# Clustered attention and spatial gating on one core: simple steps moved between ScalarE, VectorE and PSUM, and a new planned order

## The chip, the cores and the metric

The kernel runs on one core of a Trainium2 chip. The metric is the device time of one execution in microseconds; the kernel before takes 690.79 us (median of 3 runs, 690.44 to 691.78).

## What is computed

Attention in which a query sees only the keys of its own cluster, and on its output a spatial gating layer. Batch 4, 8 heads, 768 positions, head dimension 64, 16 clusters; model width 512, inner width 1024, of which u and v are 512 each. Everything goes in and out as float32.

```python
q_assign = argmax(q_n @ c_n)            # q_n, k_n, c_n: rows of unit length
k_assign = argmax(k_n @ c_n)
scores = where(q_assign == k_assign, scale * q @ k.T, -1e9)
attn = softmax(scores);  x = attn @ v   # heads side by side: [4, 768, 512]
h = relu(x @ w_in);  u, v = h[..., :512], h[..., 512:]
v_n = (v - mean(v)) / sqrt(var(v) + 1e-6)
v_s = w_spatial @ v_n + b_spatial
out = (u * v_s) @ w_out
```

## The kernel before, in words

TensorE works on float16. So that results stay close to float32, most operands are split into a high part (the value cast to float16) and a low part (what the cast lost), and products are summed from high x high, high x low and low x high.

**Pairs of heads.** The work is cut into 16 pairs of heads, four for each batch. For pair n, `prep(n)` loads keys and queries (`raw`) and values (`vraw`), splits them (ScalarE makes `hq`, line 532; VectorE subtracts to `lo`, line 538; for values lines 601 and 606), multiplies with the centroids (lines 553 to 555) and turns the products into one-hot rows on VectorE (lines 566 to 571). Two VectorE operations scale the one-hots by a penalty and write them as float16 into `ohx` (lines 577 and 578); a DMA transpose and row copies on SyncE's queue put them below the keys and queries in `hq`, so that the score matmul itself adds the mask. Sums over the values (line 621 or 613) are split into `wh` (VectorE, line 630), `w` (line 631) and `wl` (ScalarE, line 632).

`shifts(n)` multiplies scores a first time (line 662) only for their maxima, which VectorE reduces out of PSUM (line 669, 18 reductions a pair), and puts the negated maxima into further rows of `hq` (lines 680 to 684, through ScalarE, whose bias at 684 is read from a tile `flag`).

`attend(n)` goes over 2 heads x 6 key tiles: scores into a PSUM tile of 768 columns (lines 713 and 715), exp on ScalarE with a bias read from the tile `plog` (line 719, float32 `p`), the cast to float16 on ScalarE (line 721), the low part on GpSimd (line 722, one instruction over 768 columns), and the product with the values (line 727). Lines 746 to 751 normalise a head's result and split it into `xhl`; a DMA transpose makes `xT`.

**The gating layer.** `mlp(b)` follows when the four pairs of a batch are there, beside the pairs of the next batch. All its matmuls are at line 771: x with w_in to v (line 792, its statistics at 798 to 809, normalised at 811, cast to float16 by VectorE at 812, low part by GpSimd at 813) and to u (line 822); w_spatial with v_n; VectorE multiplies with u (line 832) and casts (line 833), GpSimd makes the low part (line 834), a DMA transposes it to `gT`; the product with w_out leaves through ScalarE (line 842).

**Weights.** w_in comes in eight pieces of 512 columns. It is stored as two words for each element; three VectorE operations put a word together in a PSUM accumulator (lines 477 to 479, `acc`), then ScalarE casts (line 461) and VectorE subtracts (line 462). w_out comes in eight pieces of 256 columns that take the same steps with the words put together in SBUF (`top`). w_spatial comes as float32 in twelve pieces of 384 columns.

**Order.** Nothing is issued as it is written. Each operation is entered in a plan with an engine, a cost, what it comes after, a key and in part a due time (line 195 on). `Plan.run` steps through time: whichever engine is free takes, of the operations that could start by then, the one with the lowest due time (or start) plus key, and the instruction is emitted. Each engine's queue thus has a fixed order. Four PSUM accumulators of 512 columns (`acc`) are shared by maxima, products with centroids, sums, attention results, the gating layer and w_in's words; two of 1024 (`sc`) hold scores.

Of the kernel before, what the change touches and what calls it, by code (L numbers as in the profile page):

```python
# [7 lines left out]
F32 = mybir.dt.float32  # L8
# [43 lines left out]
MM = 6  # L52
W_KEY = 7.7
WL_KEY = 0.91
WL_AT = 183.98
WL_GAP = 3.25
W_AT = 28.34
W_GAP = 5.52
PREP_KEY = 2.81
AV_KEY = 1.09  # L60
K_SC = -2.4
K_MX = -2.81
K_MAX = -0.27

TBL = 0.14
K_SH = -3.11
K_EXP = 0.71
K_HI = -1.78
K_LO = 2.77
K_RC = -1.64  # L70
K_XD = 3.66
K_X = -1.98
K_VT = -3.58
K_G = -9.5
KP0 = -16.99
KC = -30.0
# [44 lines left out]
class Op:  # L121
    __slots__ = ("eng", "cost", "fn", "after", "order", "new", "claim", "key", "at", "dma", "turn", "cols", "due", "left", "ready", "outs", "end", "seq", "alt", "s", "free")
# [14 lines left out]
class Plan:  # L137
# [24 lines left out]
    def run(self):
# [47 lines left out]
        while done < len(self.ops):  # L210
# [29 lines left out]
            if o.dma is None:  # L240
# [35 lines left out]
def kernel(  # L276
# [75 lines left out]
    r_wraw = R(wk, "wraw", [P, 512], F32, 2)  # L352
# [48 lines left out]
    m_half = op("DVE", 0.2, lambda: (V.memset(half, 0.5), V.memset(mhalf, -0.5), V.memset(plog, P_LOG * LN2), V.memset(flag[:, 0:1], -1.0), V.memset(flag[:, 1:2], -(2.0 ** -MEAN_LOG)), [V.memset(x[:, :, 2:3], LIM) for x in nms]), key=-9)  # L401
# [50 lines left out]
    def weights(jobs, at, gap, key, raws, tops, on, after=()):  # L452
        ends = []
        for m, (src, dst, n, lg, wide, cell) in enumerate(jobs):
# [4 lines left out]
            def lows(x, ld, n=n, dst=dst, sc=sc, raw=raw, cell=cell, use=()):  # L459

                h = op("ACT", 0.2 + 0.00085 * n, lambda: A.activation(out=dst()[:, 0, :], in_=x(), func=AF.Copy, scale=sc), after=ld, use=use, key=key)
                lo = op("DVE", (0.05 if n > 384 else 0.4) + 0.00125 * n, lambda: V.scalar_tensor_tensor(out=dst()[:, 1, :], in0=x(), scalar=sc, in1=dst()[:, 0, :], op0=ALU.mult, op1=ALU.subtract), after=[h], use=use, key=key)
                w_ops.setdefault(cell, []).extend([h, lo])
                ends.append(lo)
# [12 lines left out]
            x1 = op("DVE", (0.1 if n > 256 else 0.3) + 0.0011 * n, lambda raw=raw, top=top, n=n: V.tensor_scalar(out=top.t.bitcast(U32), in0=words(raw, n, 1), scalar1=3, scalar2=0x3FFFFFFF, op0=ALU.logical_shift_left, op1=ALU.bitwise_and), after=[ld], use=[raw], new=[top], key=key)  # L477
            x2 = op("DVE", (0.05 if n > 256 else 0.35) + 0.00125 * n, lambda raw=raw, top=top, n=n: V.scalar_tensor_tensor(out=top.t.bitcast(U32), in0=words(raw, n, 1), scalar=0xC0000000, in1=top.t.bitcast(U32), op0=ALU.bitwise_and, op1=ALU.bitwise_or), after=[x1], use=[raw, top], key=key)
            x3 = op("DVE", (0.05 if n > 256 else 0.35) + 0.00125 * n, lambda raw=raw, top=top, n=n: V.scalar_tensor_tensor(out=top.t.bitcast(U32), in0=words(raw, n, 0), scalar=29, in1=top.t.bitcast(U32), op0=ALU.logical_shift_right, op1=ALU.bitwise_or), after=[x2], use=[raw, top], key=key)
            lows(lambda top=top: top.t, [x3], use=[top])  # L480
# [35 lines left out]
    def prep(n):
        plan.due = due(n, DUE_PREP) if n else None
# [15 lines left out]
        for h, ld in enumerate(raws):  # L533
            if n == 1:
                o = op("ACT", 0.83, lambda h=h: A.activation(out=raw.t[:, h, :], in_=raw.t[:, h, :], func=AF.Copy, scale=QK_SCALE), after=[his[h]], use=[raw], key=KP)
                los.append(op("POOL", 1.7, lambda h=h: G_.tensor_tensor(out=lo.t[:, h, :], in0=raw.t[:, h, :], in1=hq.t[:, 0, h, :], op=ALU.subtract), after=[o], use=[raw, hq] + ([lo] if h else []), new=[] if h else [lo], key=KP))
                continue
            los.append(op("DVE", 1.4 if n else 0.96, lambda h=h: V.scalar_tensor_tensor(out=lo.t[:, h, :], in0=raw.t[:, h, :], scalar=QK_SCALE, in1=hq.t[:, 0, h, :], op0=ALU.mult, op1=ALU.subtract), after=[his[h]], use=[raw, hq] + ([lo] if h else []), new=[] if h else [lo], key=KP))  # L538
# [38 lines left out]
        k1 = op("DVE", 0.32, lambda: V.tensor_scalar(out=ohxv[:, :, 0:2], in0=oh2(0), scalar1=PEN, scalar2=None, op0=ALU.mult), after=[o_oh, last.get("oht"), c_oh], use=[misc], key=KP)  # L577
        k2 = op("DVE", 0.32, lambda: V.tensor_scalar(out=ohxv[:, :, 2:4], in0=oh2(1), scalar1=PEN, scalar2=-PEN, op0=ALU.mult, op1=ALU.add), after=[o_oh, last.get("oht"), c_oh], use=[misc], key=KP)
# [335 lines left out]
```

## Time and profile before

| what | value |
|---|---|
| median of 3 runs | 690.79 us (690.44 to 691.78) |
| the profiled execution: span from first to last instruction | 692.5 us |
| mean granted TensorE clock | 0.985 |
| TensorE busy | 637.5 us, 92% |
| VectorE busy | 482.0 us, 70% |
| ScalarE busy | 437.7 us, 63% |
| GpSimd busy | 435.3 us, 63% |
| read from HBM, written | 27.63 MB, 6.29 MB |

The profiled execution is one of its own and is not among the three runs; its span alone is above their median. In the profile's rows PE is TensorE, DVE VectorE, ACT ScalarE, POOL GpSimd and SP SyncE. A row of a group gives line, engine, operation, output and inputs with their shapes and the count; then busy time and the mean of one in ns; then the engine's idle time before them and what ended it. The chain of waits follows the work back from the last instruction, at each step to what released it. A row of the table over stretches gives the stretch, then each engine's busy time in it with its instructions, the granted TensorE clock, the share of the DMA engines and GB/s. Matmuls are pipelined and their ends modelled.

### The profile page before, as it was taken

To read this page: it belongs to the slowest core of one execution; us is meant where nothing else is said; L and a number is where in the kernel's file an instruction comes from. 1 tells how busy PE (TensorE), PEld (TensorE's weight loads), DVE (VectorE), ACT (ScalarE), POOL (GpSimd) and SP (SyncE) were. 2 spreads that over 40 slices of the span, in tenths; PEclk is the share of its full clock that TensorE was granted. 3 is DMA by queue.
4 is the path that set the end of the run, shared out by engine and by line. 5 is a ranking of instruction groups with operands and counts; after the bars stand their busy time and mean duration, and the time that the engine had idled before them with its cause. 6 is when DMAs were issued, how large, how long until landed. Compare 5 with 4: busy or idle time off the path is not lost.

```text
span 692.5 us, 16725 instructions
## 1 busy us (share of the span) xinstructions
PE 637.5 (92%) x6757; PEld 379.0 (55%) x6757; DVE 482.0 (70%) x940; ACT 437.7 (63%) x685; POOL 435.3 (63%) x305
## 2 busy tenths in 40 slices
PE   2978889999998999988799899999999999999996
PEld 1456566666555655555445556556655655544442
DVE  6999989998969889999754877558485821215210
ACT  5686889998848756678443966667673957412111
POOL 2485778998949667677363976767665966703210
PEclk9998999999999799999999999999999999999999
DMA  5567665574634467442831536262510113140223
GB/s 165 147 154 213 147 107 142 137 168 116 138 110 82 97 165 167 109 116 60 189 61 36 150 74 137 61 152 50 120 34 1 37 28 70 32 115 0 31 61 92
DMA packets 106515, 70.49 MB, mean 102 GB/s; under 512 B 90379, under 2 KB 93126, under 8 KB 106438
## 3 DMA queue, kind: packets, MB, share of 16 engines
q1 hardware_dynamic: 102694, 62.74, 40.4%
q10 hardware_dynamic: 3744, 6.69, 2.7%
q8 instruction: 53, 0.87, 0.5%
q14 instruction: 24, 0.20, 0.1%
HBM read 27.63 MB, written 6.29 MB: 49 GB/s over the span
## 4 chain that ended last, share of the span: by engine, by line
PE 60%; DVE 20%; ACT 9%; issue 5%; DMA 4%; POOL 2%; POOLq 0%; SPq 0%; ACTq 0%; DVEq 0%
PE acc L771 35%; PE acc L727 9%; DVE nm L669 8%; PE acc L662 6%; PE sc L713 5%; PE sc L715 5%; ACT p L719 4%; ACT pt L721 3%; DVE lo L538 2%; POOL pt L722 2%; DMA out_dram<-o 2%; DMA gT<-ghl 1%; ACT hq L532 1%; DVE vhl L606 1%; DVE acc L568 1%
## 5 line engine op out<-in xcount | busy, mean ns | idle before, releaser
L722 POOL TENSOR_TENSOR pt<-p,pt 128x768 f16<-128x768 f32 x192 | 329.7, 1736 | 103.1 <-ACT pt L721 50.6
L719 ACT ACTIVATE p<-sc,plog 128x768 f32<-128x768 f32 x192 | 168.9, 898 | 58.4 <-PE sc L715 53.8
L669 DVE TENSOR_REDUCE nm<-acc 128x1 f32<-128x512 f32 (+1 forms) x288 | 179.8, 683 | 12.4 <-PE acc L662 12.0
L721 ACT CAST pt<-p 128x768 f16<-128x768 f32 x192 | 155.6, 828 | 12.9 <-PE acc L727 11.1
L727 PE MATMUL acc<-vhl,pt 128*128 128x65 f16 (+1 forms) x3456 | 139.2, 196 | 7.6 <-POOL pt L722 6.9
L727 PEld LDWEIGHTS <-pt 128*128 128x128 f16 x3456 | 129.1, 99 | 30.3 <-POOL pt L722 10.1
L771 PE MATMUL acc<-win,xT 128*128 128x512 f16 x576 | 130.0, 379 | 0.0
L662 PE MATMUL acc<-hq 80*128 80x256 f16 (+1 forms) x384 | 101.1, 339 | 20.7 <-DVE nm L669 10.1
L713 PE MATMUL sc<-hq,lo 128*128 128x512 f16 (+1 forms) x384 | 95.7, 331 | 6.3 <-ACT p L719 6.1
L715 PE MATMUL sc<-hq 81*128 81x512 f16 (+1 forms) x384 | 96.0, 331 | 1.0 <-DMA hq<-sht 1.0
L771 PE MATMUL acc<-vn,wsp 128*128 128x512 f16 x432 | 96.8, 379 | 0.0
L771 PEld LDWEIGHTS <-xT 128*128 128x128 f16 x576 | 54.9, 98 | 63.2 <-issue 0.7
L771 PEld LDWEIGHTS <-wsp 128*128 128x128 f16 x432 | 41.8, 98 | 48.9 <-issue 0.2
L834 POOL TENSOR_TENSOR ghl<-u,ghl 128x512 f16<-128x512 f32 x24 | 27.7, 1156 | 64.0 <-DVE ghl L833 49.2
L832 DVE SCALAR_TENSOR_TENSOR u<-acc,bsp,u 128x512 f32<-128x512 f32 x24 | 17.9, 747 | 71.5 <-PE acc L771 71.5
L771 PE MATMUL acc<-wou,gT 128*128 128x512 f16 x288 | 65.6, 379 | 1.7 <-DMA gT<-ghl 1.7
L662 PEld LDWEIGHTS <-hq 80*128 80x128 f16 x384 | 35.3, 99 | 43.2 <-issue 25.1
L538 DVE SCALAR_TENSOR_TENSOR lo<-raw,hq 128x768 f16<-128x768 f32 x30 | 44.9, 1505 | 12.4 <-ACT hq L532 12.0
L713 PEld LDWEIGHTS <-lo 128*128 128x128 f16 x384 | 34.1, 98 | 34.9 <-issue 20.8
L715 PEld LDWEIGHTS <-hq 81*128 81x128 f16 x384 | 37.9, 99 | 27.7 <-issue 2.7
L842 ACT ACTIVATE o<-acc 128x512 f32<-128x512 f32 x24 | 14.3, 597 | 57.0 <-PE acc L771 41.2
L771 PEld LDWEIGHTS <-gT 128*128 128x128 f16 x288 | 27.7, 98 | 33.8 <-DMA gT<-ghl 2.2
(111 smaller groups left out, 628.5 us busy)
## 6 DMA issues: line engine op xcount, KB each, us to landing
raw<-in_kqT_dram SPq DMA_DIRECT2D x15, 768.0 KB
vraw<-in_vp_dram SPq DMA_DIRECT2D x16, 384.0 KB
out_dram<-o ACTq DMA_DIRECT2D x24, 256.0 KB
hq<-hq SPq DMA_DIRECT2D x15, 384.0 KB
vn<-in_w_in_dram SPq DMA_DIRECT2D x8, 512.0 KB
hq<-lo SPq DMA_DIRECT2D x16, 192.0 KB
lo<-hq SPq DMA_DIRECT2D x16, 192.0 KB
wraw<-in_wsT_dram SPq DMA_DIRECT2D x12, 192.0 KB
```

Source lines behind the costliest of these rows:

```text
L538: los.append(op("DVE", 1.4 if n else 0.96, lambda h=h: V.scalar_tensor_tensor(out=lo.t[:, h, :], in0=raw.t[:, h, :], scalar=QK_SCALE, in1= ...
L662: T.matmul(out=acc.t[:, c:c + cs.stop - cs.start], lhsT=hq.t[0:R_SH, 1, h, t * P:(t + 1) * P], rhs=hq.t[0:R_SH, 0, h, cs], start=c == 0, s ...
L669: V.tensor_reduce(out=nm.t[:, t, k:k + 1] if n == 1 else nm.t[:, t:t + n, k], in_=src, axis=AX.X, op=ALU.max, negate=True)
L713: T.matmul(out=sc.t[:, cs], lhsT=lo.t[:, h, ks], rhs=hq.t[:, 2, h, cs], start=True, stop=False)
L715: T.matmul(out=sc.t[:, cs], lhsT=hq.t[0:R_E, 0, h, ks], rhs=hq.t[0:R_E, 1, h, cs], start=False, stop=True)
L719: o = op("ACT", 0.9, lambda sc=sc, p32=p32: A.activation(out=p32.t, in_=sc.t[:, 0:S], func=AF.Exp, bias=plog, scale=SC_UNIT), after=[o, m_ ...
L721: o = op("ACT", 0.83, lambda pt=pt, p32=p32: A.copy(out=pt.t[:, 0, :], in_=p32.t), after=[o], use=[p32], new=[pt], key=K_HI)
L722: o = op("POOL", 1.72, lambda pt=pt, p32=p32: G_.tensor_tensor(out=pt.t[:, 1, :], in0=p32.t, in1=pt.t[:, 0, :], op=ALU.subtract), after=[o ...
L727: T.matmul(out=av.t[:, t * (D + 1):t * (D + 1) + w], lhsT=lhsT, rhs=rhs, skip_group_check=True, **f)
L771: T.matmul(out=acc.t, lhsT=lr[m][0], rhs=lr[m][1], start=(m == 0), stop=(m == n - 1))
L832: o = op("DVE", 0.72, lambda: V.scalar_tensor_tensor(out=u32.t, in0=acc.t, scalar=bsp[:, t:t + 1], in1=u32.t, op0=ALU.add, op1=ALU.mult), ...
L834: l = op("POOL", 1.2, lambda: G_.tensor_tensor(out=ghl.t[:, 1, :], in0=u32.t, in1=ghl.t[:, 0, :], op=ALU.subtract), after=[h], use=[u32, g ...
```

## The change

Nine edits; the rest of the diff renames costs and keys in the plan.

1. The bias of exp and of the columns at line 684 is a number in the instruction, not a tile. `plog`, `flag` and their memsets go.
2. The one-hot scalings (lines 577, 578) move from VectorE to ScalarE.
3. `wh` (line 630) moves from VectorE to ScalarE.
4. The casts to float16 of v_n (line 812) and of the gated product (line 833) move from VectorE to ScalarE.
5. w_out comes in four pieces of 512 columns, and its words are put together in a PSUM accumulator, as those of w_in.
6. The low part of P (line 722) is made in two instructions of 384 columns.
7. The plan models that GpSimd and some VectorE operations (`port`) delay each other, and has new costs for many operations.
8. Keys and due times have new values, and many operations have keys of their own (the `T_` constants) where they shared one. They set the order of every queue. The loads of w_in are entered from 83.49 us on, 7.94 apart, where it was 28.34 and 5.52; those of w_spatial and w_out from 107.13 on, where it was 183.98.
9. Places in the order of the gating layer's groups of matmuls have offsets by kind and batch.

The diff, cut:

```diff
-DUE_0 = 43.04
-DUE = 25.06
-DUE_PREP = -1.8
-DUE_MAX = -0.66
-DUE_M = 31.24
+DUE_0 = 42.66
+DUE = 22.86
+DUE_PREP = -44.39
+DUE_MAX = -8.22
+DUE_M = 29.84
...
+T_NRM = -41.72
+T_VL = -6.13
+T_G = 34.48
+T_GL = 13.67
+T_O = 23.71
...
+SUM_PE = tuple(range(4))
+K12 = True
+CAST = True
+SPLIT = 2
+WIDE = True
+WH_ACT = True
...
+                if o.port and e in shared:
+                    x = "POOL" if e == "DVE" else "DVE"
+                    o.end = max(o.end, shared[x] + c - PORT_OVER)
+                    shared[e] = o.end
...
-    r_wraw = R(wk, "wraw", [P, 512], F32, 2)
+    r_wraw = R(wk, "wraw", [P, 1024 if WIDE else 512], F32, 2)
...
-            for c0, c1 in ((0, 256), (256, 512)):
+            for c0, c1 in ((0, 512),) if WIDE else ((0, 256), (256, 512)):
...
-        weights(jobs, WL_AT, WL_GAP, WL_KEY, r_wraw, r_top, "SP", after)
+        weights(jobs, WL_AT, WL_GAP, WL_KEY, r_wraw, r_acc if WIDE else r_top, "SP", after)
...
+        for x in range(2):
+            if K12:
+                o = op("ACT", 0.34, lambda x=x: A.activation(out=ohxv[:, :, 2 * x:2 * x + 2], in_=oh2(x), func=AF.Copy, scale=PEN, bias=-PEN * x), ...)
...
-                cols.append(op("ACT", 0.31, lambda ...: A.activation(out=sx.t[:, :, R_E + c], in_=nl.t, func=AF.Relu, bias=flag[:, c:c + 1], scale=2 * u / LIM), ...))
+                cols.append(op("ACT", 0.22, lambda ...: A.activation(out=sx.t[:, :, R_E + c], in_=nl.t, func=AF.Relu, bias=-u, scale=2 * u / LIM), ...))
...
-                o = op("ACT", 0.9, lambda ...: A.activation(out=p32.t, in_=sc.t[:, 0:S], func=AF.Exp, bias=plog, scale=SC_UNIT), ...)
+                o = op("ACT", 0.81, lambda ...: A.activation(out=p32.t, in_=sc.t[:, 0:S], func=AF.Exp, bias=P_LOG * LN2, scale=SC_UNIT), ...)
...
-                o = op("POOL", 1.72, lambda ...: G_.tensor_tensor(out=pt.t[:, 1, :], in0=p32.t, in1=pt.t[:, 0, :], op=ALU.subtract), ...)
+                for q in range(SPLIT):
+                    qs = slice(q * S // SPLIT, (q + 1) * S // SPLIT)
+                    los_.append(op("POOL", 0.04 + 1.64 / SPLIT, lambda ...: G_.tensor_tensor(out=pt.t[:, 1, qs], in0=p32.t[:, qs], in1=pt.t[:, 0, qs], op=ALU.subtract), ...))
...
+                h = op(*(("ACT", 0.52) if CAST else ("DVE", 0.41)), lambda ...: (A.copy if CAST else V.tensor_copy)(out=vn[:, 0, t, :], in_=v.t), ...)
...
+            h = op(*(("ACT", 0.52) if CAST else ("DVE", 0.43)), lambda: (A.copy if CAST else V.tensor_copy)(out=ghl.t[:, 0, :], in_=u32.t), ...)
```

More of the change, by code (lines that the diff above doesn't have):

```diff
@@ L52 @@
 MM = 6
[L53 to L63, printed above, removed]
-TBL = 0.14
[L66 to L76, printed above, removed]
+W_KEY = 30.08
+WL_KEY = -7.61
+WL_AT = 107.13
+WL_GAP = -13.01
+W_AT = 83.49
+W_GAP = 7.94
+PREP_KEY = -10.19
+AV_KEY = -8.06
+K_SC = 10.69
+K_MX = 0.75
+K_MAX = -1.94
+TBL = 0.14
+K_SH = -11.45
+K_EXP = 25.11
+K_HI = 11.58
+K_LO = -1.1
+K_RC = 19.97
+K_XD = -22.15
+K_X = -30.89
+K_VT = -34.94
+K_G = 26.47
+KP0 = -94.77
+KC = -140.0
+T_LO = 0.55
+T_QA = -21.72
+T_LG = -8.78
+T_AM = -5.57
+T_OT = 46.02
+T_ROW = 4.57
+T_V = -21.13
+T_SV = -28.66
+T_VA = 3.34
+T_SA = -5.56
+T_SB = 2.69
+T_UO = -8.08
+T_PO = 58.41
+T_CONT = -120.66
+T_BN = -20.31
+T_NRM = -41.72
[3 more added lines that the diff above has]
+T_O = 23.71
+T_B1 = 12.24
+T_B2 = 9.87
+T_B3 = 1.32
+T_Q1 = 11.16
+T_Q2 = 4.64
+T_Q3 = 0.25
+T_Q0 = 7.9
+T_Z0 = -6.97
+T_Z1 = -11.3
+T_Z2 = 12.6
+LO_POOL = (1,)
+VL_POOL = (0, 1)
+SUM_PE = tuple(range(4))
+WS_POOL = False
+O_BUFS = 1
+K12 = True
+CAST = True
+SPLIT = 2
+WIN_POOL = ()
+WIDE = True
+WH_ACT = True
 class Ring:
@@ L121 @@
 class Op:
-    __slots__ = ("eng", "cost", "fn", "after", "order", "new", "claim", "key", "at", "dma", "turn", "cols", "due", "left", "ready", "outs", "end", "seq", "alt", "s", "free")
+    __slots__ = ("eng", "cost", "fn", "after", "order", "new", "claim", "key", "at", "dma", "turn", "cols", "due", "left", "ready", "outs", "end", "seq", "alt", "s", "free", "port")
 LAG = {"PE": 0.2, "ACT": 0.034, "DVE": 0.034, "POOL": 0.034, "SP": 0.0, "NONE": 0.0}
@@ L148, in ring, with op @@
         return r
-    def op(self, eng, cost, fn, after=(), use=(), new=(), claim=(), key=0.0, at=0.0, dma=None, turn=False, cols=0, alt=None, due=None):
+    def op(self, eng, cost, fn, after=(), use=(), new=(), claim=(), key=0.0, at=0.0, dma=None, turn=False, cols=0, alt=None, due=None, port=None):
         o = Op()
         o.due = self.due if due is None else due
+        o.port = eng == "POOL" and dma is None if port is None else port
         o.eng, o.cost, o.fn, o.key, o.at, o.dma, o.turn, o.cols, o.alt = eng, cost, fn, key, at, dma, turn, cols, alt
@@ L184, in run @@
         columns = {}
+        shared = {"DVE": 0.0, "POOL": 0.0}
         def arm(o):
@@ L400 @@
     ld_i = op("SP", 0.6, lambda: nc.sync.dma_start(out=idt(), in_=ident), use=[scratch], dma=0.2, key=KC)
-    m_half = op("DVE", 0.2, lambda: (V.memset(half, 0.5), V.memset(mhalf, -0.5), V.memset(plog, P_LOG * LN2), V.memset(flag[:, 0:1], -1.0), V.memset(flag[:, 1:2], -(2.0 ** -MEAN_LOG)), [V.memset(x[:, :, 2:3], LIM) for x in nms]), key=-9)
+    m_half = op("DVE", 0.2, lambda: (V.memset(half, 0.5), V.memset(mhalf, -0.5), [V.memset(x[:, :, 2:3], LIM) for x in nms]), key=-9)
     def fill():
@@ L575, in oh2 @@
             return misc.t[:, cs].rearrange("p (t a h c) -> p t a h c", a=2, h=2, c=C)[:, :, a]
[L577 to L578 removed]
+        k2 = None
+        for x in range(2):
+            if K12:
+                o = op("ACT", 0.34, lambda x=x: A.activation(out=ohxv[:, :, 2 * x:2 * x + 2], in_=oh2(x), func=AF.Copy, scale=PEN, bias=-PEN * x), after=[o_oh, last.get("oht"), c_oh], use=[misc], key=KA)
+            else:
+                o = op("DVE", 0.32, lambda x=x: V.tensor_scalar(out=ohxv[:, :, 2 * x:2 * x + 2], in0=oh2(x), scalar1=PEN, scalar2=-PEN * x, op0=ALU.mult, op1=ALU.add), after=[o_oh, last.get("oht"), c_oh], use=[misc], key=KA)
+            k1, k2 = k2 if x else None, o
         if n == 0:
@@ L583, in prep @@
         else:
-            tr = last["oht"] = sp(lambda: nc.sync.dma_start_transpose(oht.t, ohx.rearrange("p t x c -> p (t x c)")), 0.67, after=[k1, k2], new=[oht], turn=True, key=KP - 2)
+            tr = last["oht"] = sp(lambda: nc.sync.dma_start_transpose(oht.t, ohx.rearrange("p t x c -> p (t x c)")), 0.67, after=[k1, k2], new=[oht], turn=True, key=KP + T_OT)
         rows = []
@@ L683, in shifts @@
                 u = 2.0 ** (-MEAN_LOG * c)
-                cols.append(op("ACT", 0.31, lambda nl=nl, sx=sx, c=c, u=u: A.activation(out=sx.t[:, :, R_E + c], in_=nl.t, func=AF.Relu, bias=flag[:, c:c + 1], scale=2 * u / LIM), after=[o, c_sh, m_half], use=[nl, sx], key=K_SH))
+                cols.append(op("ACT", 0.22, lambda nl=nl, sx=sx, c=c, u=u: A.activation(out=sx.t[:, :, R_E + c], in_=nl.t, func=AF.Relu, bias=-u, scale=2 * u / LIM), after=[o, c_sh, m_half], use=[nl, sx], key=K_SH))
             if n == 0 and h == 0:
@@ L762, in mlp, with acc_group @@
         plan.due = None
-        def acc_group(n, pairs, after, pos, claim=(), step=MM, more=None):
+        def acc_group(n, pairs, after, pos, claim=(), step=MM, more=None, off=0.0):
             acc = r_acc.new()
             prev = None
+            off += DUE_W + (T_Z0, T_Z1, T_Z2, 0.0)[b]
             for c0 in range(0, n, step):
@@ L777, in xTb, with proj @@
             return xTs[b % 2]
-        def proj(t, c0, pos, claim):
+        def proj(t, c0, pos, claim, off=0.0):
             hf = 1 if c0 else 0
-            acc, o = acc_group(3 * NCT, lambda: [(xTb()[:, k, t, xi, :], win[:, wi, k, c0:c0 + DF]) for xi, wi in terms for k in range(NCT)], xdone[b] + w_ops[("win", hf)], pos, claim)
+            acc, o = acc_group(3 * NCT, lambda: [(xTb()[:, k, t, xi, :], win[:, wi, k, c0:c0 + DF]) for xi, wi in terms for k in range(NCT)], xdone[b] + w_ops[("win", hf)], pos, claim, off=off)
             xread.setdefault(b, []).append(o)
@@ L797, in v_tile @@
             st = r_st.new()
-            o = op("DVE", 0.66, lambda: V.bn_stats(out=st.t, in_=v32.t), after=[o], use=[v32], new=[st], key=1)
+            o = op("DVE", 0.66, lambda: V.bn_stats(out=st.t, in_=v32.t), after=[o], use=[v32], new=[st], key=T_BN)
             o = op("DVE", 0.08, lambda: V.bn_aggr(out=mv.t[:, k, :], in_=st.t), after=[o], use=[st] + ([mv] if k else []), new=[] if k else [mv], key=0)
@@ L807, in v_tile @@
[L807 to L809 removed]
+            o = op("DVE", 0.18, lambda: V.tensor_tensor(out=y2.t, in0=y.t, in1=y.t, op=ALU.mult), after=[o], use=[y], new=[y2], key=0, port=True)
@@ L814, in v_tile @@
+                h = op(*(("ACT", 0.52) if CAST else ("DVE", 0.41)), lambda t=t, v=v: (A.copy if CAST else V.tensor_copy)(out=vn[:, 0, t, :], in_=v.t), after=[o] + vn_read[t], use=[v], key=T_NRM, port=True)
+                l = op("POOL", 1.3, lambda t=t, v=v: G_.tensor_tensor(out=vn[:, 1, t, :], in0=v.t, in1=vn[:, 0, t, :], op=ALU.subtract), after=[h], use=[v], key=T_VL)
                 normed.extend([h, l])
@@ L832, in s_tile @@
             o = op("DVE", 0.72, lambda: V.scalar_tensor_tensor(out=u32.t, in0=acc.t, scalar=bsp[:, t:t + 1], in1=u32.t, op0=ALU.add, op1=ALU.mult), after=[o, u_ops[t]] + w_ops["bsp"], use=[acc, u32], key=K_G)
-            h = op("DVE", 0.43, lambda: V.tensor_copy(out=ghl.t[:, 0, :], in_=u32.t), after=[o], use=[u32], new=[ghl], key=0)
-            l = op("POOL", 1.2, lambda: G_.tensor_tensor(out=ghl.t[:, 1, :], in0=u32.t, in1=ghl.t[:, 0, :], op=ALU.subtract), after=[h], use=[u32, ghl], key=-0.5)
+            h = op(*(("ACT", 0.52) if CAST else ("DVE", 0.43)), lambda: (A.copy if CAST else V.tensor_copy)(out=ghl.t[:, 0, :], in_=u32.t), after=[o], use=[u32], new=[ghl], key=T_G, port=True)
+            l = op("POOL", 1.2, lambda: G_.tensor_tensor(out=ghl.t[:, 1, :], in0=u32.t, in1=ghl.t[:, 0, :], op=ALU.subtract), after=[h], use=[u32, ghl], key=T_GL)
             return op("SP", 1.2, lambda: nc.sync.dma_start_transpose(gT.t, ghl.t.rearrange("p a d -> p (a d)")), after=[l], use=[ghl], new=[gT], dma=0.9, turn=True)
@@ L839, in p_tile @@
             o32 = r_o32.new()
-            acc, o = acc_group(3 * NDT, lambda: [(gT.t[:, gi * NDT + k, :], held["wou"][:, wi, k, :]) for gi, wi in terms for k in range(NDT)], [tr] + w_ops["wou"], pos, ())
+            acc, o = acc_group(3 * NDT, lambda: [(gT.t[:, gi * NDT + k, :], held["wou"][:, wi, k, :]) for gi, wi in terms for k in range(NDT)], [tr] + w_ops["wou"], pos, (), off=T_PO)
             gT.users.append(o)
-            o = op("ACT", 0.57, lambda: A.activation(out=o32.t, in_=acc.t, func=AF.Copy, scale=2.0 ** -(G_LOG + WOUT_LOG)), after=[o], use=[acc], new=[o32], key=-0.7)
+            o = op("ACT", 0.57, lambda: A.activation(out=o32.t, in_=acc.t, func=AF.Copy, scale=2.0 ** -(G_LOG + WOUT_LOG)), after=[o], use=[acc], new=[o32], key=T_O)
             op("ACT", 0.06, lambda: A.dma_start(out=out[b, t * P:(t + 1) * P, :], in_=o32.t), after=[o], use=[o32], dma=0.8, key=0)
```

135 lines of the change are left out of this document (75 added, 60 removed).

## The prediction

> **What bounds the kernel now.** I read the page first, for the span and the costliest groups, then the chain of waits and the busy table over four stretches, cut where its character changes.
>
> ```profile
> span 692.5 us, 16725 instructions
> PE 60%; DVE 20%; ACT 9%; issue 5%; DMA 4%; POOL 2%; POOLq 0%; SPq 0%; ACTq 0%; DVEq 0%
> ```
> ```profile
> core 0: us, PE busy (x) PEld busy (x) DVE busy (x) ACT busy (x) POOL busy (x), PEclk, DMA share, GB/s
> 0.00:40.00 40.00, 24.39 (x255) 14.53 (x255) 32.35 (x89) 25.04 (x36) 16.78 (x25) 1.00 0.50 145
> 40.00:166.00 126.00, 110.44 (x1601) 77.11 (x1602) 119.88 (x221) 110.04 (x177) 101.24 (x63) 0.96 0.67 156
> 166.00:400.00 234.00, 216.64 (x2334) 129.11 (x2331) 193.94 (x353) 158.25 (x253) 159.45 (x104) 0.98 0.47 112
> 400.00:692.50 292.50, 286.01 (x2575) 158.25 (x2573) 135.78 (x279) 144.34 (x223) 157.87 (x114) 1.00 0.30 65
> ```
>
> The chain is 60% TensorE and 20% VectorE (138 us). The stretches say where. From 40 to 166 us (attention alone, pairs 0 to 4) VectorE is busy 119.88 of 126 us; it is the bound, with ScalarE (110) and GpSimd (101) close behind, and TensorE waits. From 166 to 400 TensorE is busy 217 of 234 and VectorE 194: each waits for the other in turn. After 400 TensorE is busy 286 of 292.5, and no other engine reaches 55%; there only a shorter TensorE stream would help, and the change leaves every matmul as it is. So what counts is what comes off VectorE before 400 us, and what ScalarE and GpSimd can bear before 166.
>
> **The change part by part.** VectorE first, by its groups in the stretch 40 to 166, and the one place on the chain where the subtraction into lo met no GpSimd work:
>
> ```profile
> L538 DVE SCALAR_TENSOR_TENSOR lo<-raw,hq 128x768 f16<-128x768 f32 x10 | 14.7, 1483 | 0.8 <-ACT hq L532 0.8
> L606 DVE SCALAR_TENSOR_TENSOR vhl<-vraw,vhl 128x768 f16<-128x768 f32 x4 | 5.3, 1335 | 0.0
> L462 DVE SCALAR_TENSOR_TENSOR win<-acc,win 128x512 f16<-128x512 f32 x8 | 5.3, 686 | 0.1
> L478 DVE SCALAR_TENSOR_TENSOR acc<-vn,acc 128x512 uint32<-128x512 uint32 x7 | 4.7, 692 | 0.0
> L477 DVE TENSOR_SCALAR acc<-vn 128x512 uint32<-128x512 uint32 x7 | 4.7, 688 | 0.0
> L479 DVE SCALAR_TENSOR_TENSOR acc<-vn,acc 128x512 uint32<-128x512 uint32 x7 | 4.7, 696 | 0.0
> L577 DVE TENSOR_SCALAR ohx<-acc 128x192 f16<-128x192 f32 x5 | 1.7, 348 | 0.0
> L578 DVE TENSOR_SCALAR ohx<-acc 128x192 f16<-128x192 f32 x5 | 1.7, 347 | 0.0
> L630 DVE TENSOR_SCALAR wh<-acc 2x128 f16<-2x128 f32 (+1 forms) x5 | 1.4, 275 | 1.9 <-PE acc L614 1.9
> ```
> ```profile
> 7.02 0.95 DVE lo L538
> ```
>
> Both one-hot scalings (1.7 + 1.7) and wh (1.4) leave VectorE: 4.8 us. The subtraction takes 1.48 us here against 0.95 us alone: 10 x 0.53 + 4 x (1.335 - 0.95) = 6.9 us of waiting for GpSimd's running instruction. With GpSimd's 1.7 us pieces cut in two, the rest of a running piece is half as long, so I take half, 3.5 us (bounds 0, if the other half takes its place at once, and 6.9). Sum 8.3 us of 119.88, off an engine that is 95% busy. ScalarE and GpSimd must follow, so I take **-7 us** (0 to -8). Loading w_in later (from 28 to 83 us) moves its 22 us of VectorE work inside this stretch, not out of it; I count nothing for it, though pairs 1 and 2 should run shorter and 3 and 4 longer.
>
> The same for 166 to 400:
>
> ```profile
> L538 DVE SCALAR_TENSOR_TENSOR lo<-raw,hq 128x768 f16<-128x768 f32 x12 | 18.9, 1579 | 2.1 <-ACT hq L532 1.8 <-PE acc L771 0.2
> L462 DVE SCALAR_TENSOR_TENSOR wsp<-wraw,wsp 128x384 f16<-128x384 f32 x12 | 11.3, 938 | 2.0 <-ACT wsp L461 2.0
> L606 DVE SCALAR_TENSOR_TENSOR vhl<-vraw,vhl 128x768 f16<-128x768 f32 x6 | 9.3, 1543 | 0.0
> L478 DVE SCALAR_TENSOR_TENSOR top<-wraw,top 128x256 uint32<-128x256 uint32 x8 | 9.0, 1120 | 0.1
> L462 DVE SCALAR_TENSOR_TENSOR wou<-top,wou 128x256 f16<-128x256 f32 x8 | 7.1, 886 | 0.5 <-ACT wou L461 0.5
> L479 DVE SCALAR_TENSOR_TENSOR top<-wraw,top 128x256 uint32<-128x256 uint32 x8 | 5.9, 735 | 0.1
> L812 DVE CAST vn<-v 128x512 f16<-128x512 f32 x12 | 4.6, 422 | 0.0
> L477 DVE TENSOR_SCALAR top<-wraw 128x256 uint32<-128x256 uint32 x8 | 4.3, 536 | 0.1
> L833 DVE CAST ghl<-u 128x512 f16<-128x512 f32 x6 | 2.7, 455 | 0.9 <-DMA gT<-ghl 0.9
> L577 DVE TENSOR_SCALAR ohx<-acc 128x192 f16<-128x192 f32 x6 | 2.1, 342 | 0.0
> L578 DVE TENSOR_SCALAR ohx<-acc 128x192 f16<-128x192 f32 x6 | 2.0, 338 | 0.0
> ```
>
> w_out costs 9.0 + 7.1 + 5.9 + 4.3 = 26.3 us as eight pieces in SBUF. As four 512-wide pieces through PSUM it is what w_in costs, 4 x (0.688 + 0.692 + 0.696 + 0.686) = 11.0: -15.3. The casts leave: -7.3. One-hot and wh (6 x 0.275): -5.7. Half the waiting of lo, vhl and wsp (12 x 0.63 + 6 x 0.59 + 12 x 0.25, where 0.25 is the excess of a 384-wide piece over the 512-wide w_in one): 14.1 / 2 = 7. Sum 35 us of 194, or 18%. TensorE is idle 17.4 us here, and that caps the gain, but for the clock (0.98: 4.7 us more if it stays full). I take **-14 us**, the middle between -7 (each of the 35 us counts only by VectorE's 20% share of the chain) and -22.
>
> The loads of w_out on SyncE's queue become four of twice the size, the same bytes, at a DMA share of 0.47: nothing. The w_out pieces now each hold one of the four PSUM accumulators for some 4 us beside the matmuls: 16 us of bank time in 234 x 4, taken as nothing (2 us if each stops TensorE 0.5 us). The one-hot scalings and wh now stand in ScalarE's line; for them wait, on SyncE's queue, the transpose of ohx and the row copies, then the next pair's maxima. I count nothing, since that pair is prepared beside the one before (126 us for five, 25 each); with that cover gone it is one exp and one cast for each of 16 pairs, 28 us (rows below).
>
> ScalarE and GpSimd, by the page and the groups of forms:
>
> ```profile
> L722 POOL TENSOR_TENSOR pt<-p,pt 128x768 f16<-128x768 f32 x192 | 329.7, 1736 | 103.1 <-ACT pt L721 50.6
> L719 ACT ACTIVATE p<-sc,plog 128x768 f32<-128x768 f32 x192 | 168.9, 898 | 58.4 <-PE sc L715 53.8
> L721 ACT CAST pt<-p 128x768 f16<-128x768 f32 x192 | 155.6, 828 | 12.9 <-PE acc L727 11.1
> L842 ACT ACTIVATE o<-acc 128x512 f32<-128x512 f32 x24 | 14.3, 597 | 57.0 <-PE acc L771 41.2
> ```
> ```profile
> L751 POOL TENSOR_TENSOR xhl<-xn,xhl 128x384 f16<-128x384 f32 x32 | 32.7, 1023 | 5.2 <-ACT xhl L750 5.1
> L684 ACT ACTIVATE shx<-nl,flag 128x6 f16<-128x6 f32 x64 | 15.9, 308 | 0.0
> L681 ACT ACTIVATE shx<-nl 128x6 f16<-128x6 f32 x32 | 7.2, 226 | 3.2 <-DVE nl L680 3.1
> L461 ACT ACTIVATE wsp<-wraw 128x384 f16<-128x384 f32 x12 | 6.2, 518 | 0.8 <-DMA wraw<-in_wsT_dram 0.7
> ```
>
> A bias read from a tile costs 308 - 226 = 82 ns at equal shape, so the 192 exps and 64 columns give back 256 x 0.082 = 21 us. Added: 32 scalings of 192 columns at 0.37 (bounds 0.226 and 0.518) = 12, 16 wh at 0.27 = 4, 48 casts at 0.6 (the 512-wide row) = 29. Net +24 us, but not evenly: in 40 to 166 it is -56 x 0.082 - 20 x 0.082 + 10 x 0.37 + 5 x 0.27 = -1.2, so ScalarE does not become the bound there; after 166 it has the room.
>
> A rule of the Trainium skill speaks against this move: ScalarE: Activation LUTs, Rules for kernel authors, has copies and other simple elementwise work on VectorE, which is up to about three times faster per element. The trace agrees on the sign (0.42 to 0.46 us on VectorE, 0.6 on ScalarE); by it the casts lose 48 x 0.16 = 8 us of engine time, and the sum would be 8 us higher if all of it lay on the path.
>
> GpSimd's half piece has no row. From below it is half of 1736, 868 ns; from above the 384-wide xhl, 1023, though that row holds lock waits too. I take 0.93, nearer the lower since the 768-wide row is the same operation on the same operands: 2 x 0.93 - 1.736 = +0.12 us a tile, +23 us over the kernel, +7 in 40 to 166 (101 to 108 of then 119: still not the bound).
>
> Ahead of 40 us some VectorE work goes (first w_in piece, three memsets): **-1**. After 400, TensorE idles 6.5 us; the last tile's cast is 0.15 us longer on the path, the other order may close some gaps: **-2** (0 to -5). Sum -7 - 14 - 1 - 2 = -24 us off the profiled 692.5, which is 1.7 above the median 690.79 (0.2%): about **667 us**.
>
> All engine orders are new, too, and no trace shows them; I price that by the rivals.
>
> **The rivals.** *TensorE takes it all.* VectorE's relief and the new order close nearly all gaps between 40 and 400: -15.6 - 17.4, with 4.7 of clock and 5 after 400: -43, 648 us. For it: VectorE loses 43 us there; against: three engines at 80% and over rarely mesh in fixed queues.
>
> *GpSimd becomes the bound before 166.* At 1023 a half it gains 60 x 0.31 = 19 us, 120 of 126: the first gain is gone and waits of pt pass into 166 to 400 (159 + 21 of 234, half the gain): -10, 681 us. The Trainium skill says why it could be (GPSIMD Engine Reference, Instruction dispatch): each instruction passes a software dispatcher on all its cores, so two halves pay twice.
>
> *ScalarE's queue holds TensorE up: slower.* Each of 48 casts now stands in one line with exps and casts of 0.898 + 0.828 = 1.73 us; behind it wait GpSimd's subtraction, the transposes and the matmuls of the projection. If over 14 casts (24 / 1.73) come one such pair late where TensorE has nothing else, it decides; at 28 the result is +24, 715 us. Against: after 600 us no exp is left, and before it TensorE has two streams.
>
> *The biases are not immediate*, but put in a tile again: ScalarE loses 21 us of room, the stretch to 166 gains 2 rather than 7: 672 us.
>
> **How the numbers follow.** Forecast (655 to 678) 0.52; TensorE takes it all (below 655) 0.15; GpSimd the bound or another shrinking of the gain (678 to 689) 0.18; tile biases 0.02, inside the forecast's range; slower 0.10, and 0.03 that relief and new waits cancel. The measurement of this kernel tells about 0.2%, 1.4 us. Faster 0.87, same 0.03, slower 0.10. Cutting 0.09 below and 0.11 above leaves 647 to 689.
>
> **What would show it.** Right: lo near 1.2 us; exp near 0.816; no w_out group under 512 wide; VectorE below 112 us in the time that pairs 0 to 4 take; that stretch some 7 us shorter and the next 14. Wrong: halves of 1.0 us and GpSimd's waits gone from before pt; ScalarE named before ghl and vn with TensorE idle behind; a first stretch as long as before, in which case ScalarE or the order, not VectorE's work, was the bound.

## The result and the profile after

The changed kernel takes 670.24 us (median of 4 runs, 667.57 to 671.38) beside 690.96 of the kernel before: ratio 0.9687, 95% interval 0.9661 to 0.9713, or 20.7 us less. The forecast was 667. The profiled execution has a span of 669.6 us, its page beginning so:

```profile
span 669.6 us, 16891 instructions
PE 629.5 (94%) x6757; PEld 375.9 (56%) x6757; DVE 428.8 (64%) x825; ACT 452.8 (68%) x777; POOL 456.9 (68%) x497
PE 58%; DVE 9%; ACT 5%; DMA 4%; issue 2%; POOL 0%; POOLq 0%; ACTq 0%; DVEq 0%
```

VectorE's busy time fell from 482 to 429 us. Its 9% of the chain must not be set beside the 20% of before: after, the chain's shares add up to 78% only, because it is followed back to 137 us and no further. From 139 us on, VectorE's pieces of the chain add up to some 62 us before and 62 us after. Where the time went shows in the table over stretches, with the second cut moved to 162 us so that the same cuts serve both; first the kernel before, then the changed one:

```profile
0.00:40.00 40.00, 24.39 (x255) 14.53 (x255) 32.35 (x89) 25.04 (x36) 16.78 (x25) 1.00 0.50 145
40.00:162.00 122.00, 107.06 (x1540) 74.62 (x1541) 118.07 (x217) 106.53 (x170) 98.87 (x62) 0.96 0.66 153
162.00:400.00 238.00, 220.03 (x2390) 131.60 (x2389) 195.75 (x358) 161.76 (x259) 161.83 (x106) 0.98 0.48 114
400.00:692.50 292.50, 286.01 (x2575) 158.25 (x2573) 135.78 (x279) 144.34 (x223) 157.87 (x114) 1.00 0.30 65
```
```profile
0.00:40.00 40.00, 23.08 (x216) 14.05 (x217) 30.39 (x81) 24.53 (x41) 13.96 (x27) 0.94 0.51 147
40.00:162.00 122.00, 109.21 (x1594) 75.90 (x1593) 114.98 (x201) 108.54 (x191) 110.82 (x120) 0.95 0.70 156
162.00:400.00 238.00, 234.46 (x2591) 139.88 (x2587) 172.49 (x323) 170.18 (x299) 174.72 (x185) 1.00 0.51 114
400.00:669.60 269.60, 262.78 (x2367) 146.07 (x2365) 110.94 (x222) 149.57 (x248) 157.39 (x168) 1.00 0.31 68
```

TensorE's idle time (length less PE busy) was 15.6, 14.9, 18.0 and 6.5 us; now it is 16.9, 12.8, 3.5 and 6.8, so 15 us less in all, nearly all of it in the third stretch: 201 matmuls more fit between 162 and 400 us. The other 8 of the 23 us by which the span is shorter are busy time: the same 6757 matmuls keep TensorE busy for 629.5 us and not 637.5. The granted clock rose in the third stretch (0.98 to 1.00) and fell ahead of it (1.00 to 0.94 and 0.96 to 0.95), so it is not shown to be the reason. TensorE's waits there by name, before and after:

```profile
PE acc L662 <- DVE nm L669: 4.3, 6, 2.1
PE acc L727 <- POOL pt L722: 4.0, 7, 1.0
PE acc L662 <- ACT o L842: 3.4, 2, 1.8
PE acc L662 <- DVE ohx L578: 1.7, 2, 1.6
PE sc L713 <- ACT p L719: 1.6, 5, 0.5
PE acc L662 <- DVE u L832: 1.2, 1, 1.2
```
```profile
PE acc L847 <- DMA xT<-xhl: 0.9, 1, 0.9
PE sc L784 <- ACT p L790: 0.6, 2, 0.5
PE acc L733 <- DVE nm L740: 0.6, 3, 0.2
PE acc L733 <- DVE wou L523: 0.5, 1, 0.5
PE acc L693 <- DVE vs L692: 0.3, 1, 0.3
```

No one wait went; many short ones did, on three engines. The prices of the parts, from the changed kernel's groups:

```profile
L796 POOL TENSOR_TENSOR pt<-p,pt 128x384 f16<-128x384 f32 x384 | 355.6, 959 | 48.0 <-issue 20.1
L790 ACT ACTIVATE p<-sc 128x768 f32<-128x768 f32 x192 | 152.4, 809 | 23.9 <-PE sc L786 15.3
L909 ACT CAST ghl<-u 128x512 f16<-128x512 f32 x24 | 14.8, 617 | 55.2 <-DVE u L908 36.5
```
```profile
L604 DVE SCALAR_TENSOR_TENSOR lo<-raw,hq 128x768 f16<-128x768 f32 x30 | 39.2, 1313 | 4.0 <-ACT hq L598 3.8
L646 ACT ACTIVATE ohx<-acc 128x192 f16<-128x192 f32 x32 | 9.0, 327 | 8.5 <-DVE acc L637 8.4
L523 DVE SCALAR_TENSOR_TENSOR wou<-acc,wou 128x512 f16<-128x512 f32 x4 | 2.7, 684 | 0.1
```

### The profile page after: what moved, and what is told of

Same layout as the page of the kernel before. It is cut to its first block, busy times and chain, and to the rows that moved or that the text cites. A ratio compares the mean times of both kernels' runs of the same rounds, so it can differ in the third digit from the quotient of the medians.

```text
span 669.6 us, 16891 instructions
## 1 busy us (share of the span) xinstructions
PE 629.5 (94%) x6757; PEld 375.9 (56%) x6757; DVE 428.8 (64%) x825; ACT 452.8 (68%) x777; POOL 456.9 (68%) x497
## 4 chain that ended last, share of the span: by engine, by line
PE 58%; DVE 9%; ACT 5%; DMA 4%; issue 2%; POOL 0%; POOLq 0%; ACTq 0%; DVEq 0%
PE acc L847 34%; PE acc L802 9%; PE sc L784 5%; PE sc L786 5%; PE acc L733 4%; DVE nm L740 3%; ACT p L790 2%; DMA out_dram<-o 1%; DVE lo L604 1%; DMA gT<-ghl 1%; ACT pt L792 1%; DMA xT<-xhl 1%; DVE wsp L523 1%; DMA vraw<-in_vp_dram 1%; DVE st L874 1%
## 5 line engine op out<-in xcount | busy, mean ns | idle before, releaser
L796 POOL TENSOR_TENSOR pt<-p,pt 128x384 f16<-128x384 f32 x384 | 355.6, 959 | 48.0 <-issue 20.1
L740 DVE TENSOR_REDUCE nm<-acc 128x1 f32<-128x512 f32 (+1 forms) x288 | 181.8, 680 | 29.3 <-PE acc L733 28.0
L790 ACT ACTIVATE p<-sc 128x768 f32<-128x768 f32 x192 | 152.4, 809 | 23.9 <-PE sc L786 15.3
L802 PEld LDWEIGHTS <-pt 128*128 128x128 f16 x3456 | 127.1, 98 | 24.5 <-issue 4.3
L802 PE MATMUL acc<-vhl,pt 128*128 128x65 f16 (+1 forms) x3456 | 135.8, 194 | 1.3 <-POOL pt L796 1.1
L733 PE MATMUL acc<-hq 80*128 80x256 f16 (+1 forms) x384 | 94.8, 333 | 8.5 <-DVE nm L740 4.2
L909 ACT CAST ghl<-u 128x512 f16<-128x512 f32 x24 | 14.8, 617 | 55.2 <-DVE u L908 36.5
L826 POOL TENSOR_TENSOR xhl<-xn,xhl 128x384 f16<-128x384 f32 x32 | 30.6, 958 | 28.2 <-ACT xhl L825 28.2
L733 PEld LDWEIGHTS <-hq 80*128 80x128 f16 x384 | 32.6, 98 | 27.8 <-issue 9.6
```

Of the source, the lines that this page charges most:

```text
L733: T.matmul(out=acc.t[:, c:c + cs.stop - cs.start], lhsT=hq.t[0:R_SH, 1, h, t * P:(t + 1) * P], rhs=hq.t[0:R_SH, 0, h, cs], start=c == 0, s ...
L740: V.tensor_reduce(out=nm.t[:, t, k:k + 1] if n == 1 else nm.t[:, t:t + n, k], in_=src, axis=AX.X, op=ALU.max, negate=True)
L790: o = op("ACT", 0.81, lambda sc=sc, p32=p32: A.activation(out=p32.t, in_=sc.t[:, 0:S], func=AF.Exp, bias=P_LOG * LN2, scale=SC_UNIT), afte ...
L796: los_.append(op("POOL", 0.04 + 1.64 / SPLIT, lambda pt=pt, p32=p32, qs=qs: G_.tensor_tensor(out=pt.t[:, 1, qs], in0=p32.t[:, qs], in1=pt. ...
L802: T.matmul(out=av.t[:, t * (D + 1):t * (D + 1) + w], lhsT=lhsT, rhs=rhs, skip_group_check=True, **f)
L826: xls.append(op("POOL", 1.0, lambda xn=xn, hs=hs: G_.tensor_tensor(out=xhl.t[:, :, 1, hs], in0=xn.t, in1=xhl.t[:, :, 0, hs], op=ALU.subtra ...
```

## The experiments

Each ran beside the kernel before on its chip; ratios are to that (95% intervals in brackets). The changed kernel stands at 0.9687, so 0.001 is 0.7 us. The first theory (A) was the prediction's: the work taken off VectorE is the gain. The first rival (B): the order of the queues is. "In place" means that the plan is left alone and only the instruction issued differs, so that every queue keeps its order.

**1. The edits in the old order.** In the kernel before:

```diff
-V.tensor_scalar(out=ohxv[:, :, 0:2], ...)
+A.activation(out=ohxv[:, :, 0:2], in_=oh2(0), func=AF.Copy, scale=PEN)
...
-bias=plog
+bias=P_LOG * LN2
-G_.tensor_tensor(out=pt.t[:, 1, :], ...)
+[G_.tensor_tensor(out=pt.t[:, 1, qs], ...) for qs in (slice(0, 384), slice(384, 768))]
-V.tensor_copy(out=ghl.t[:, 0, :], in_=u32.t)
+A.copy(out=ghl.t[:, 0, :], in_=u32.t)
```

> The kernel before with its plan, and so every queue's order, unchanged; only what is issued differs: number biases, one-hot scalings, wh and the two casts on ScalarE, the low part of P in two halves right behind each other. The words of w_out stay in SBUF, 256 wide. Theory A (the work taken off VectorE is what the change gains): most of the 20.7 us come, 673 to 680 us, VectorE's busy time falls from 482 to 445 or less. Rival B (the new order is what gains, the edits only shift load): 686 us or more. Rival C (both are needed, an edit inside an order that was planned without it runs into waits): 691 or more, with new waits on ScalarE before ghl, vn and the transposes of ohx.

688.62 us, 0.9957 (0.9935 to 0.9978): 3 us. VectorE's load fell as A wants, to 440 us, and hardly any time came of it. Theory A in this form falls; so does C's loss. Two of its longest waits: GpSimd's idle time in which it waits for nothing that the profile shows (23.8 us in the kernel before), and ScalarE's at the place where its cast now waits for VectorE.

```profile
POOL pt L722 <- issue: 39.1, 19, 3.8
ACT ghl L833 <- DVE u L832: 38.7, 15, 4.2
```

The second is no mark of the old order: the changed kernel has 36.5 us of the same wait (the row of L909 above).

**2. The new order without the edits.** In the changed kernel, in place: `plog` and `flag` again, one-hots, wh and casts on VectorE, the low part whole. w_out stays wide.

```diff
-(A.copy if CAST else V.tensor_copy)(out=ghl.t[:, 0, :], in_=u32.t)
+V.tensor_copy(out=ghl.t[:, 0, :], in_=u32.t)
...
-los_.append(op("POOL", ..., lambda ...: G_.tensor_tensor(out=pt.t[:, 1, qs], ...), ...))
+los_.append(op("POOL", ..., None if q else lambda ...: G_.tensor_tensor(out=pt.t[:, 1, :], ...), ...))
```

> The changed kernel's order of issue, with the edits undone in what is issued: tile biases, one-hot scalings, wh and casts on VectorE, the low part of P whole; w_out stays 512 wide with its words in PSUM. Theory A: little of the gain is left, 683 to 690 us. Rival B: most of it is left, 670 to 677 us. Rival C: 690 or more, since this order was planned with the edits.

683.30 us, 0.9860 (0.9826 to 0.9895): at the lower end of A's range, but 9.7 us of the gain stay without these edits. In the order planned for them the edits are worth 0.0173, 12 us; in the old order 3. And lo, beside whole low parts of 768, is down as far as with halves, by the order alone:

```profile
L606 DVE SCALAR_TENSOR_TENSOR lo<-raw,hq 128x768 f16<-128x768 f32 x30 | 37.5, 1257 | 1.8 <-ACT hq L600 1.7
```

**3. Each edit undone by itself, in place.** Casts on VectorE, the whole low part, tile biases, one-hots and wh on VectorE, each as in the diffs above.

> The changed kernel with the casts of v_n and of the gated product on VectorE again, at the same places of the order. Theory A: VectorE gets 21 us back, two thirds of it after 162 us, where TensorE is busy all the time: 671 to 674 us. The rival that ScalarE's line holds the gating layer up (0.62 us a cast against 0.45, and exps ahead of it): faster, 665 to 669 us. No difference (669 to 671.5) would say that neither engine is on the path there.

674.21 us, 0.9740 (0.9710 to 0.9769): +3.7 us, about what A has. The interval just touches that of the changed kernel (up to 0.9713).

> The changed kernel with the low part of P as one GpSimd instruction of 768 columns again. Theory A (halves shorten VectorE's waits for GpSimd): lo back from 1.31 to about 1.5 us, vhl from 1.12 to 1.4, VectorE 8 to 10 us busier, 673 to 677 us. Rival (two halves cost GpSimd more than they give; its groups went from 329.7 to 355.6 us, and from 40 to 162 it is busy 110.8 of 122): 663 to 668 us, the gain before 162.

675.14 us, 0.9749 (0.9721 to 0.9776): +4.3 us. The size is A's, the reason is not: VectorE's busy time stayed (429.8 us), lo rose only to 1.38 us, vhl to 1.13. That two halves cost GpSimd more than they give is refuted. Why halves help is open: the plan enters the products with the values behind the second half, and no run let them start after the first.

> The changed kernel, same order, with the biases of exp and of the shift columns read from tiles again. ScalarE loses 192 x 0.089 + 64 x 0.09 = 23 us. Theory A (ScalarE is near its limit only before 162 us, 108.5 of 122): 6 us more work there, little after: 673 to 676 us. Rival (ScalarE's room is what the order lives on all along): 678 us or more. Rival (ScalarE is never on the path): 669 to 671.

674.62 us, 0.9750 (0.9727 to 0.9772): +4.4 us, as A has it.

> The changed kernel, same order, with the one-hot scalings and wh on VectorE again: VectorE gets 16 us back, ScalarE loses 13. Theory (VectorE is the path before 162 us): 5 us of that lie there, 672 to 675 us. Rival (ScalarE's line is the path there, and the one-hots wait in it): 665 to 669 us. The edits undone one at a time would then sum to 4.4 (biases), 3.7 (casts), 4.3 (halves) and this one, beside 13 us for all at once.

671.70 us, 0.9716 (0.9690 to 0.9743): +2.0 us, which the intervals don't tell from nothing; neither theory's figure.

The four sum to 14 us beside 12 for all at once: undone in a given order, each is a small, separate loss.

**4. w_out in narrow pieces, and the plan without its port model.**

```diff
-WIDE = True
+WIDE = False
```

> The changed kernel with w_out in eight pieces of 256 columns and their words in SBUF again (the order after about 200 us is planned anew with the same keys). VectorE gets 12 to 15 us back between 200 and 300 us. Theory A: 674 to 680 us. Rival (TensorE is busy there all the time and hides it): 669 to 672 us.

679.54 us, 0.9825 (0.9796 to 0.9854): +9.5 us, though VectorE's busy time rose by 7.9 us only (428.8 to 436.7). The order differs, too, so this is not the price of the pieces alone.

```diff
-        o.port = eng == "POOL" and dma is None if port is None else port
+        o.port = False
```

> The changed kernel with the plan's model of VectorE and GpSimd delaying each other switched off; all else, the costs and keys too, as it is, so the order differs where that model moved an operation. Theory (the model is what makes the new order good): 676 us or more, with lo back at 1.4 us or more. Rival (costs and keys make it, the model is one perturbation among others): 667 to 674 us, lo near 1.3.

676.94 us, 0.9807 (0.9773 to 0.9841): +8.3 us at the median. lo, though, is shorter than in the changed kernel (1.183 against 1.313), so a shorter lo is not what the port model brought:

```profile
L604 DVE SCALAR_TENSOR_TENSOR lo<-raw,hq 128x768 f16<-128x768 f32 x30 | 35.2, 1183 | 5.4 <-ACT hq L598 5.4
```

**5. The same edit, planned.** This gave theory D: the keys fit one list of operations, and the order that comes of them is worth more than any edit.

```diff
-CAST = True
+CAST = False
```

> The changed kernel with the two casts on VectorE as in the run with the casts back (674.2 us beside 692.1 of before, 0.974), but this time the plan knows it, and lays a new order with the same keys. Theory D (the keys fit one list of operations and no other; the order is worth more than any single edit): 690 us or more, the edit the same and only the order different. Rival (keys of this kind make a good order for any near list): 672 to 677 us.

691.96 us, 1.0019 (1.0000 to 1.0037). The casts sit on VectorE as in the run that took 674; the keys are the same; the plan knows of it and lays another order, and the whole gain is gone.

**6. One key.** No operation differs from the changed kernel:

```diff
-K_SC = 10.69
+K_SC = 11.0
```

> The changed kernel with one key other: K_SC, the place of the score matmuls, 11.0 for 10.69. Every operation and every edit is as in the changed kernel; only the planned order of the queues differs. Theory D (the order is worth as much as all the edits, and only this one order has it): 685 us or more. Rival (the edits carry the gain, and neighbouring orders keep it): 669 to 674 us.

707.93 us, 1.0222 (1.0198 to 1.0247): 37 us over the changed kernel, 16 over the kernel before, with every edit in place. Its stretches, the last two of four:

```profile
162.00:400.00 238.00, 225.79 (x2348) 132.29 (x2347) 157.64 (x300) 158.95 (x278) 160.04 (x169) 0.99 0.45 105
400.00:708.00 308.00, 292.11 (x2662) 163.28 (x2660) 131.68 (x253) 165.65 (x277) 175.16 (x189) 0.97 0.31 68
```

TensorE idles 12 and 16 us in them, with VectorE busy 66% and 43% of the time, and ScalarE and GpSimd below 70%. What this order does shows at the end. Here are the stretches from the end of the last exp to the end of the run, first of the changed kernel, then of this one:

```profile
575.10:669.60 94.50, 88.91 (x458) 40.87 (x456) 17.64 (x44) 22.73 (x38) 21.87 (x22) 1.00 0.25 59
```
```profile
581.00:707.80 126.80, 119.44 (x580) 54.40 (x580) 20.54 (x48) 27.29 (x47) 29.17 (x29) 0.97 0.23 54
```

The last exp ends 6 us later, and 32 us more are left behind it: 580 matmuls instead of 458, most of them of the gating layer (216 products with w_spatial instead of 140). In experiment 5 it is the same: 125.5 us and 580 matmuls are left, although its exps end at 564.6 us, before the changed kernel's. In every other run, the kernel before too, 94 to 95 us are left.

**7. Old order, biases and halves alone.** Experiment 1 with nothing moved between engines.

```diff
-A.copy(out=ghl.t[:, 0, :], in_=u32.t)
+V.tensor_copy(out=ghl.t[:, 0, :], in_=u32.t)
```

> The kernel before, same order, with number biases and the low part of P in two halves, but nothing moved between engines. Theory C (in an order that was planned without them the moved operations make ScalarE wait: 38.7 us before ghl in the run of the edits in the old order): faster than that run's 0.9957 of before, 681 to 686 us. Rival (the old order has no place for any relief): 687 to 692 us.

687.79 us, 0.9939 (0.9919 to 0.9958): no better than all edits (0.9957), so the moves' new waits on ScalarE are not what spoils experiment 1. The old order makes little of any relief: biases and halves give 4.2 us together here, and 4.4 and 4.3 us one by one in the changed kernel's order.

**8. No edit, but an order of its own.** The kernel before in every operation, planned with the changed kernel's costs, port model and separate keys; the key and due values were searched anew for this list of operations, and 57 of them are other than the changed kernel's. Some of them:

```diff
-DUE_0 = 42.66
+DUE_0 = 43.72
-WL_KEY = -7.61
+WL_KEY = 24.41
-KP0 = -94.77
+KP0 = -79.26
...
```

> The kernel before in its operations (tile biases, one-hot scalings, wh and casts on VectorE, the low part of P whole, w_out in eight narrow pieces), but planned with the changed kernel's costs and separate keys, and these keys searched anew for this list of operations. Theory D (a fitted order is worth about half of the gain by itself, the edits the other half): 676 to 684 us. Rival (the edits carry the gain): 686 us or more. Rival (the order is all of it): 673 us or less.

672.79 us, 0.9724 (0.9687 to 0.9761). Rival B is left: an order of its own is worth 19 us without any edit, and the changed kernel, with the edits and its own order, is 0.0037 lower, 2.6 us, which the intervals do not tell from nothing. Its page, its two middle stretches and lo:

```profile
PE 624.0 (93%) x6757; PEld 371.7 (55%) x6757; DVE 469.3 (70%) x940; ACT 438.9 (65%) x685; POOL 428.5 (64%) x305
```
```profile
40.00:162.00 122.00, 107.23 (x1681) 75.43 (x1680) 117.44 (x225) 112.51 (x179) 105.28 (x67) 1.00 0.75 162
162.00:400.00 238.00, 232.06 (x2473) 137.01 (x2472) 193.76 (x371) 164.80 (x264) 160.03 (x109) 1.00 0.47 111
```
```profile
L606 DVE SCALAR_TENSOR_TENSOR lo<-raw,hq 128x768 f16<-128x768 f32 x30 | 41.9, 1400 | 4.0 <-ACT hq L600 3.8
```

VectorE is as busy from 162 to 400 us as in the kernel before (193.8 against 195.8), and still TensorE idles 6 us there and not 18.

Idling is not all of it. The profiled executions, with the same 6757 matmuls in each:

| kernel | span, us | TensorE busy | TensorE idle | granted clock |
|---|---|---|---|---|
| before | 692.5 | 637.5 | 55.0 | 0.985 |
| changed | 669.6 | 629.5 | 40.1 | 0.987 |
| one key (6) | 707.8 | 644.6 | 63.2 | 0.977 |
| order of its own (8) | 671.4 | 624.0 | 47.4 | 1.000 |

In experiment 8 idling gives 8 of the 21 us by which the span is shorter; the other 13 are busy time, at a clock that was full throughout. Over its six runs the mean clock is 0.995, over the eleven of the kernel before on that chip 0.988; among the six a clock 0.01 higher goes with 2.6 us less time, among the eleven with 4.5. By an estimate from these, 2 to 3 of the 19 us go with the clock. Whether the order brings the fuller clock or chance does, no run here shows.

## Why the prediction was right and its reason was not

**The size** was right: 24 us forecast, 20.7 measured. That it came out is luck, as the next paragraph shows. **The place** was half right: -14 us for 166 to 400 stands beside 14.4 us less TensorE idling from 162 to 400; the cap of 17.4 us was the useful number.

**The reason** failed at the step "what counts is what comes off VectorE before 400 us". A busy engine off which 35 us are taken and a neighbour that idles 17 us looked like cause and effect; experiment 8 has the same load on VectorE between 162 and 400 us and two thirds of the idling there gone, experiment 6 has the load taken off and the idling back (12 us), and experiment 1 takes off 42 us of VectorE's busy time, 19 of them before 400 us, for 3 us. Busy shares say how much work an engine has, not that its work stands in the way: between 162 and 400 the waits were short ones on VectorE, GpSimd and ScalarE. The new order was put at nothing but a share of -2 and at the rivals. It is the term that was mis-sized: an order made for the old operations measured -19 (experiment 8), and the changed kernel's own order without the edits, its wide w_out kept, -10 (experiment 2). The edits' terms, -21 to 400 us, were too large: 3 us in the old order, 12 in the changed kernel's without w_out's part, and 2.6 beside an order of the old operations' own. The two errors cancelled.

**0 to 40, -1:** wrong in sign. Pair 0's first exp comes 3.9 us later. Some 2 us of that are later scores (TensorE ends them at 31.0 us, where before the exp could start at 29.1); the other 2 it stands on ScalarE behind a pair's one-hot scalings and the casts that make a `hq`. Before, then after:

```profile
29.09 0.90 ACT L719 ACTIVATE p<-sc,plog 128x768 f32<-128x768 f32 x1 [3.67 <-PE sc L715]
```
```profile
31.06 0.55 ACT L646 ACTIVATE ohx<-acc 128x192 f16<-128x192 f32 x2 [1.74 <-DVE acc L637]
31.50 1.57 ACT L598 ACTIVATE hq<-raw 128x768 f16<-128x768 f32 x2
32.96 1.51 ACT L790 ACTIVATE p<-sc 128x768 f32<-128x768 f32 x2
```

**To 166, -7:** pairs 0 to 4 take 4 us less, counted from the start: their last exp begins at 160.2 us and not 164.4. VectorE is busy 115.0 us between 40 and 162, where under 112 was the sign. The part put down to the halves came to nothing in sum: the ten subtractions into lo in that stretch take 1.506 us in the mean, before 1.483; nine of them take 1.26 and one takes 3.73. TensorE idles 2.1 us less there, after 1.3 more before 40.

**After 400, -2:** 0 (idle 6.5 and 6.8 us).

**Prices.** exp 0.809 (0.816 forecast); a cast on ScalarE 0.617 (0.6), a one-hot scaling 0.327 (0.37); a half 0.959 (0.93); w_out 2.7 us for the last of its steps, as w_in. lo 1.31, where 1.2 was forecast and put down to the halves. In place the halves do shorten it, from 1.51 to 1.23 in the old order (experiment 7) and from 1.38 to 1.31 in the changed kernel's, but it moves as much without them: with whole parts it is 1.40 in the order of experiment 8 and 1.26 in experiment 2.

**Rivals.** That ScalarE's queue holds TensorE up: casts on VectorE again in place made it slower, not faster. A cast is dearer on ScalarE (0.617 us; on VectorE 0.42 and 0.47 in the kernel before, 0.48 and 0.60 in that run), and still the time in that order is 3.7 us shorter. The prediction cites the Trainium skill against this move (ScalarE: Activation LUTs, Rules for kernel authors): its row puts relu, max, min, add and mul on VectorE, up to about three times faster per element in bf16, and does not name copies or casts. The one-hot scaling is such a mul, but from float32 in PSUM; it takes 0.35 us on VectorE and 0.327 on ScalarE, so in this case VectorE is not the faster one. GpSimd as the bound: refuted by the whole low part. Tile biases again: refuted, exp has no second input. TensorE takes it all: true from 162 to 400 alone.

What stays open: which feature of an order makes it good, beyond TensorE's idling and what is left behind the last exp; what the clock has to do with it; and whether the edits are worth anything with the best order for each list, since neither search was complete.

## What to carry to other kernels

Where queues have a fixed order and three or four engines are busy over 60%, test an edit twice: in place, with the order kept, and with an order laid anew for it; here an edit undone in place cost 2 to 4 us, while one undone with an order laid anew lost the whole gain, and a searched order without any edit had nearly all of it. Before work is moved off the busiest engine, see whether its neighbour's idling is one long wait or many short ones: here it was many short ones on several engines, and another order closed most of them. Look also at what an order leaves for the end: in the two orders that lost the gain, 31 to 32 us more stood behind the last exp. And a change that brings an edit together with new keys is to be compared with new keys alone.

## What was not expected

One key moved by 0.31, no operation changed, costs 37 us (5.6%), more than all the edits and the first order together had gained; in the profiled executions 32 of 38 us stand behind the last exp. A GpSimd instruction over 384 columns has a mean of 0.959 us, so two take 1.92 where one of 768 took 1.70 in the same order; GpSimd's busy time in them is 355.6 us and not 322.1, and the kernel with them is 4.3 us faster all the same.
